# The first 64 score bursts of a transformer block in another order: four query groups per key tile, projections by row tile, the norm in pieces

## The chip, the cores and the metric

The kernel runs on one core of one Trainium2 chip. The metric is the device time of one execution in microseconds. Before the change it is 1097.61 us, the median of 3 runs (1097.25 to 1097.75).

## What is computed

One pre-norm transformer block in bf16, with x of 2048 rows by 1024 columns. Attention has 32 query heads of 32 columns and one key and value head that all of them share; the second half is a gated feed-forward part of width 3584. Cut to what matters:

```python
def attention(x):
    q = (x @ wq).reshape(B, S, 32, 32).transpose(0, 2, 1, 3)
    k, v = x @ wk, x @ wv
    scores = einsum("bhqd,bkd->bhqk", q, k) * 32 ** -0.5
    o = einsum("bhqk,bkd->bhqd", softmax(scores), v)
    return o.transpose(0, 2, 1, 3).reshape(B, S, 1024) @ wo

def ffn(x):
    return (sigmoid(x @ w_gate) * (x @ w_up)) @ w_down

h  = x + attention(layernorm(x))
h2 = h + ffn(layernorm(h))
```

## The kernel before, in words

**Tiles and bursts.** The rows are 16 tiles of 128. Eight chunks of four heads make up the 1024 query columns (a "q" below is 128 columns, four heads). A *unit* is two row tiles (256 rows); there are eight units, and the feed-forward part goes by unit too. The scores of one row tile are worked in *bursts*: in one burst TensorE makes four score matmuls, one per head on its own 32 rows of the array, into two pairs of PSUM banks of `S_ps` (L727 to L752). ScalarE then takes the exponential of each pair in one instruction of 128 x 1024 (`one_exp`, L757 to L772). There are 512 bursts, so 1024 exponentials. `ORDER` (L128) lists the groups of eight bursts; there are 64 groups `g`.

**Narrow and wide groups.** The groups from the ninth on are wide: one burst is one key tile against four q of one row tile (512 columns per matmul), and a group is one half of the keys. The first eight groups (row tiles 0 and 1) are narrow: a burst is two key tiles against two q (eight matmuls of 256 columns, L744 to L752), and a group goes over all keys.

**Probabilities times V, and the sums.** `pv_group` (narrow, L979) and `pv_wide` (L885) multiply the probabilities by V, four heads on four column strips of the array. The sum of each row of probabilities comes in one of two ways. For groups 0 to 2 (`G_SUM = 3`) TensorE multiplies the same probabilities by ones (L1017). For the others VectorE first adds tiles pairwise (`add_pair`, L843; `run` and `merge`, L861 and L870, or L820 and L832 where wide), and TensorE multiplies only the last result by ones (L999, or L933 where wide). VectorE then copies the product out, inverts the sum through two 32x32 transposes and multiplies (L1038 to L1050, or L905, L908, L955 to L966).

**The head.** Up to the 25th burst the order is written out by hand: the first three groups go together (`HG = 3`), each taking key tiles 2p and 2p+1 in turn, and the strings of `HEAD` (L125) say what is put between the bursts: V projections, query projections, the norm of a row tile, pieces of the first product with V. `k_group` (L569) projects two key tiles at a time (256 columns) and ScalarE copies the result out (L576). `vq_group` (L610) projects two q for one row tile, or V for two tiles; the copies of query groups 0 and of some others go to ScalarE (L632, L652), the others and V's to VectorE (L639, L636). `q_group` (L645) projects one q for 256 or 512 rows (L654). Where TensorE would wait, `keep_busy` (L334) puts in matmuls of zeros (L346).

**The first layernorm** is made tile by tile: statistics (`ln1_stats`, L427: two of L431 and one of L436), subtraction (L458) and multiplication (L463) on VectorE, the power on GpSimd, then a DMA transpose on SP's queue (L553). The calls are written out in the head, two to three tiles ahead of what the bursts need. `LOADS` (L425) says after which tile's transpose SP's queue loads which further tile of x; x tiles 4 to 7 and the first three pieces of wq are asked for at the start (L270 to L273).

**The main loop** (L1583 to L1690) runs from the 26th burst on. It keeps a clock for each engine from costs in the code (L135 and the second argument of each `inc`), and picks the next thing for TensorE: the next burst once the exponentials before it are done by that clock, else products with V as `PV_PLAN` allows, else `next_group` (L1352): the output projection with wo (L1104), then query projections, then gate, up and down of the feed-forward part. All of these use the two banks of `X_ps`; a group takes a bank in `open_group` and gives it back when it has been copied out (`run_item`, L350 to L365). VectorE's work that may wait stands in a list (`put`, L1066), from which `dve_fill` (L1072) takes what fits before the next copy.

**Where the probabilities wait** for V: a ring of 18 tiles in `Pr`, and in the head also parts of `hact`, `wo` and `QT` that are not yet in use (`p_tile`, L708). wo is loaded, and the later columns of `QT` are written, when the products with V have come 16 bursts far (L1590, L648).

Of the kernel before, what the change touches and what calls it, by code (L numbers as in the profile page):

```python
# [8 lines left out]
F32 = mybir.dt.float32  # L9
# [75 lines left out]
def bass_sequential_preLN__grouped_kv_mqa__glu_gated_glu__prompt_kernel(  # L85
# [43 lines left out]
    ORDER += [(t_, i_) for t_ in range(2, NT) for i_ in range(NQ // 2)]  # L129
    UNITS = [[t_, t_ + 1] for t_ in range(0, NT, TPQ)]  # L130
# [3 lines left out]
    WD_AT, WD_GAP, WD_LATE = 6, 4, 10  # L134
# [5 lines left out]
    with ExitStack() as es:  # L140
# [99 lines left out]
        def _(unused):  # L240
# [70 lines left out]
            I_US, I_MAX = 4.0, 210  # L311

            def by_columns(g):
# [10 lines left out]
                return pe_mode[0] == "s" and (more or n < NQC * NQ and k[0] >= min(BPG * (n + 1) + 1, NB - (n == NQC * NQ - 1)))  # L324
# [100 lines left out]
            LOADS = {3: (8,), 4: (9,), 5: ("q3", 10), 6: (11,), 7: (12, 13), 9: (14,), 11: (15,)}  # L425
# [43 lines left out]
            def ln1_out(t):  # L469
                xnT_read[t] = xnT_val[t] = transposed(sp, xnT_tile(t), xn(t), t % 4, xn_val[t])  # L470
                for i in LOADS.get(t, ()):
                    if i == "q3":
                        load_wq(3, 768, 256)
                    else:
                        load_x(i)
# [93 lines left out]
            def k_group(p, mid=None):  # L569
                c0 = 2 * p * P  # L570

                def evac(bank, tick):
                    if mid is not None:
                        mid()
                    need(act, tick)
                    k_val[p] = c_act.inc(act.activation(out=kT4[:, c0:c0 + 256], in_=bank[:, 0:256], func=ACTF.Copy), 0.33, 0.1)  # L576
                    return k_val[p]
                items = mm_list([(wk4[:, dt, :], xnT[:, p, dt, :]) for dt in range(DT)],
# [1143 lines left out]
```

## Time and profile before

| What | Number |
|---|---|
| median of 3 runs | 1097.61 us |
| span of the profiled execution, first to last instruction | 1094.1 us |
| TensorE, matmuls | 1075.0 us, 98% of the span |
| ScalarE | 1007.0 us, 92% |
| VectorE | 897.4 us, 82% |
| GpSimd | 65.8 us, 6% |
| HBM read and written | 161.61 MB and 4.19 MB |

The profile holds one execution, whose span is 1094.1 us; the time of a run is taken around the whole program, and the median of the runs is 3.5 us above the span. Rows of the profile give the line of the kernel, the engine, what is written and read, the shapes, the count, the busy time and the mean of one. A matmul's duration contains its way through the array, which the next one overlaps: sixteen matmuls in a row take far less than sixteen durations, and what counts is the distance from start to start.

### The profile page before, as it was taken

To read this page: it belongs to the slowest core of one execution; us is meant where nothing else is said; L and a number is where in the kernel's file an instruction comes from. 1 tells how busy PE (TensorE), PEld (TensorE's weight loads), DVE (VectorE), ACT (ScalarE), POOL (GpSimd) and SP (SyncE) were. 2 spreads that over 40 slices of the span, in tenths; PEclk is the share of its full clock that TensorE was granted. 3 is DMA by queue.
4 is the path that set the end of the run, shared out by engine and by line. 5 is a ranking of instruction groups with operands and counts; after the bars stand their busy time and mean duration, and the time that the engine had idled before them with its cause. 6 is when DMAs were issued, how large, how long until landed. Compare 5 with 4: busy or idle time off the path is not lost. (4 is left out here: it accounts for less than half of the span.)

```text
span 1094.1 us, 33732 instructions
## 1 busy us (share of the span) xinstructions
PE 1075.0 (98%) x14751; PEld 632.2 (58%) x14804; DVE 897.4 (82%) x1494; ACT 1007.0 (92%) x1155; POOL 65.8 (6%) x136
## 2 busy tenths in 40 slices
PE   8999999999999999999999999999999999999999
PEld 7564466644666356643666347653666447653884
DVE  7769997889988989799989899898888899798321
ACT  6999999999999999999999999999999999999110
POOL 4500110100000000000000000000000000000000
PEclk9999999999999999999999999999999999999999
DMA  9842528950976549670997719670697509872570
GB/s 209 163 116 81 127 70 244 258 131 24 245 212 191 118 109 250 197 205 21 242 244 206 154 31 275 193 179 25 167 263 215 126 22 269 232 197 71 149 175 20
DMA packets 332418, 175.84 MB, mean 161 GB/s; under 512 B 39536, under 2 KB 326512, under 8 KB 332272
## 3 DMA queue, kind: packets, MB, share of 16 engines
q1 hardware_dynamic: 326464, 163.47, 58.8%
q0 software_dynamic: 2544, 9.44, 2.7%
q8 instruction: 116, 1.90, 0.8%
q10 hardware_dynamic: 3264, 0.79, 0.4%
q14 instruction: 30, 0.25, 0.1%
HBM read 161.61 MB, written 4.19 MB: 152 GB/s over the span
## 5 line engine op out<-in xcount | busy, mean ns | idle before, releaser
L770 ACT ACTIVATE Pr<-S_ps 128x1024 bf16<-128x1024 f32 x992 | 943.6, 1204 | 3.2 <-PE S_ps L747 1.4
L820 DVE TENSOR_TENSOR pairs<-Pr 128x1024 bf16<-128x1024 bf16 x446 | 303.8, 684 | 28.7 <-ACT Pr L770 27.9
L832 DVE TENSOR_TENSOR pairs<-pairs 128x1024 bf16<-128x1024 bf16 x390 | 269.0, 690 | 11.4
L328 PE MATMUL X_ps<-QT,wgu 128*128 128x128 bf16 (+1 forms) x2263 | 209.5, 243 | 1.3 <-DMA wgu<-in_B_w_gate_dram 1.2
L328 PEld LDWEIGHTS X_ps<-QT,wgu 128*128 128x128 bf16 x2263 | 163.9, 98 | 39.5 <-issue 25.9
L737 PE MATMUL S_ps<-QT,kT 32*128 32x512 bf16 x1792 | 176.8, 385 | 1.5 <-ACT Pr L770 0.9
L328 PE MATMUL X_ps<-zone,hact 128*128 128x512 bf16 (+2 forms) x652 | 150.0, 371 | 4.4 <-issue 3.8
L328 PE MATMUL X_ps<-QT 128*128 128x128 bf16 (+1 forms) x1652 | 153.1, 242 | 0.2
L328 PEld LDWEIGHTS X_ps<-QT 128*128 128x128 bf16 x1652 | 119.9, 98 | 25.8 <-issue 15.6
L1253 ACT ACTIVATE gu<-X_ps 128x512 f32<-128x512 f32 x112 | 86.9, 776 | 45.7 <-PE X_ps L328 45.6
L737 PEld LDWEIGHTS S_ps<-QT,kT 32*128 32x128 bf16 x1792 | 45.0, 91 | 135.1 <-ACT Pr L770 123.9
L1274 DVE SCALAR_TENSOR_TENSOR hact<-gu,X_ps 128x512 bf16<-128x512 f32 x112 | 76.6, 684 | 48.7 <-PE X_ps L328 47.5
L894 PE MATMUL X_ps<-Pr,V 128*32 128x512 bf16 x1792 | 114.8, 381 | 0.4
L328 PEld LDWEIGHTS X_ps<-zone,hact 128*128 128x128 bf16 x686 | 59.2, 98 | 73.9 <-issue 18.5
L894 PEld LDWEIGHTS X_ps<-Pr,V 128*32 128x32 bf16 x1792 | 41.5, 96 | 48.5 <-issue 14.0
L330 PE MATMUL X_ps<-zone,hact 128*32 128x512 bf16 x952 | 61.3, 380 | 0.0
L328 PE MATMUL X_ps<-zone 128*128 128x512 bf16 (+3 forms) x506 | 60.2, 264 | 1.0 <-ACT kT L576 0.4
L399 POOL CAST mean<-mv 128x1 f32<-128x1 bf16 x28 | 8.7, 310 | 816.1 <-DVE mv L1145 804.2
L328 PE MATMUL X_ps<-wo,QT 128*128 128x512 bf16 x213 | 53.7, 380 | 1.4 <-issue 0.6
L330 PE MATMUL X_ps<-QT,wgu 128*32 128x256 bf16 (+1 forms) x1636 | 50.8, 264 | 0.0
L328 PEld LDWEIGHTS X_ps<-zone 128*128 128x128 bf16 x506 | 32.6, 97 | 22.5 <-issue 7.9
L330 PEld LDWEIGHTS X_ps<-QT,wgu 128*32 128x32 bf16 x1636 | 38.9, 97 | 11.2 <-issue 6.6
(108 smaller groups left out, 720.8 us busy)
## 6 DMA issues: line engine op xcount, KB each, us to landing
wgu<-in_B_w_up_dram SPq DMA_DIRECT2D x81, 512.0 KB, 5.6
wgu<-in_B_w_gate_dram SPq DMA_DIRECT2D x72, 512.0 KB, 5.7
QT<-in_B_w_gate_dram SPq DMA_DIRECT2D x57, 512.0 KB, 5.5
QT<-in_B_w_up_dram SPq DMA_DIRECT2D x48, 512.0 KB, 6.7
zone<-in_B_w_down_dram POOLq DMA_DIRECT2D x14, 512.0 KB, 6.2
out_dram<-hx SPq DMA_DIRECT2D x31, 128.0 KB, 1.7
hx<-in_A_x_dram SPq DMA_DIRECT2D x15, 256.0 KB, 2.8
Pr<-in_B_w_gate_dram SPq DMA_DIRECT2D x5, 512.0 KB, 7.2
```

What stands on the lines that cost most here:

```text
L328: return pe.matmul(out, lhsT=lhsT, rhs=rhs, start=start, stop=stop, skip_group_check=main[0])
L330: ins = pe.matmul(out[DH * j:DH * (j + 1)], lhsT=lhsT[:, DH * j:DH * (j + 1)], rhs=rhs, start=start, stop=stop, tile_position=(0, DH * j), ...
L399: return c_pool.inc(pool.tensor_copy(out=mean[:, i:i + 1], in_=mv[:, i:i + 1, 0]), 0.2)
L737: ins = pe.matmul(S_ps[:, ((2 * k + j // 2) % 3) * 2 + j % 2, :], lhsT=kT4[DH * j:DH * (j + 1), kt * P:(kt + 1) * P], rhs=QT[DH * j:DH * ( ...
L770: c_e.inc(act.activation(out=p_tile(k, n % 2), in_=S_ps[:, 2 * pr:2 * pr + 2, :].rearrange("p a (b q) -> p (a b) q", q=QC), func=ACTF.Exp, ...
L820: slot_use[x] = c_dve.inc(dve.tensor_tensor(out=dst(x), in0=p_tile(k - 1, hh), in1=p_tile(k, hh), op=ALU.add), T_ADD, 0.08)
L832: slot_use[x] = slot_use[y] = c_dve.inc(dve.tensor_tensor(out=pairs[:, x, :], in0=pairs[:, x, :], in1=pairs[:, y, :], op=ALU.add), T_ADD, ...
L894: ins = pe.matmul(bank[DH * j:DH * (j + 1), :], lhsT=V[:, kt, :], rhs=p_tile(k, j // 2)[:, j % 2 * 2:j % 2 * 2 + 2, :], start=b == 0, stop ...
L1253: tanh_val[n] = c_act.inc(act.activation(out=slot, in_=bank, func=ACTF.Tanh, scale=0.5), T_TANH, 0.1)
L1274: gu_read[n] = c_dve.inc(dve.scalar_tensor_tensor(out=hact[:, 2 * fs[0]:2 * fs[0] + ft, r0:r0 + len(ts) * P], in0=slot.rearrange("p (a b) ...
```

## The change

**Order of the bursts.** All groups are wide now. Groups 0 to 3 are row tiles 0 and 1 against the first half of the keys, for q 0 to 3 and q 4 to 7. They take each key tile in turn (after two key tiles each at the very start); groups 4 to 7 are the second half of the keys, one group after the other. Products with V of groups 0 to 3 come in two chunks of four bursts each, the sums likewise, and `OLP` and `OLS`, which lie in parts of `hact` and `hx`, hold what has been added up until the second half is there.

**Sums.** `SUM_PLAN = "ppppdddp"`: of the first eight groups, TensorE makes the sums of five by itself, and VectorE adds for three.

**Projections.** Keys are projected tile by tile (128 columns) and copied out by VectorE, but for the first two; queries of row tiles 0 and 1 two q at a time; rows 256 to 511 one q at a time. No table: `TODO` is a list of priorities, of which `head_group` takes the first whose inputs are there by the kernel's clock. The main loop runs from the first burst on, and `keep_busy` is not reached in it.

**Norm.** The layernorm of tiles 2 to 15 stands in VectorE's list in four pieces per tile. x tiles 4 and 5 are loaded after tile 2's transpose, 6 and 7 after tile 3's, and so on; the fourth piece of wq is asked for at the start.

**Ring and constants.** The places for the probabilities are given out by a first-in-first-out list over `Pr`, `wo` and `QT` (9, 4 and 4 bursts). The plans and thresholds of the main loop have other values.

```diff
-    NEAR = 1
-    PV_PLAN = "aaacabaaacadaaaAadaaaAaAdAadaaaaadbbaaaDbaaaaaaacbbaaaaDaabCbAaa"
-    WO_PLAN = "aaaaaaba"
-    PV_HOLD = 1.0
-    BANK_WAIT = 0.15
-    G_SUM, NPB = 3, 4
-    HG = 3
-    HEAD = ['u', 'Vu', 'L', '', 'VULu', 'u', 'VPP', 'wL', 'LzPULz', 'zPLz', 'W', 'LzP', 'PPzL', 'VVL', 'PPV', '', 'UPP', 'UP', 'PV', 'U', 'PU', '', '', '']
+    NEAR = 2
+    PV_PLAN = "BDaeeaaaAbbaaBbaAEeAababaAbBeAaaEAAaeDbdeaAbbbaEDabAAabaAaaabaAaacbcabDa"
+    WO_PLAN = "bbabaaaa"
+    PV_HOLD = 0.75
+    BANK_WAIT = 0
+    G_SUM, HCH, HB0 = 4, 4, 2
+    LN_LEAD = 2
+    SUM_PLAN = "ppppdddp"
     K_BUSY = 10
-    HEAD_U = [5, 6, 7, 4]
-    ORDER = [(0, 0), (0, 1), (0, 2), (1, 0), (0, 3), (1, 1), (1, 2), (1, 3)]
+    TODO = ["k1", "k0", "q1a", "q1b", "q0a", "q0d", "q0c", "q0b", "k2", "q1d", "k5", "k4", "ka", "v1", "v0", "k7",
+            "q1c", "v3", "v2", "k3", "k6", "kc", "kf", "kd", "kb", "ke", "v4", "v7", "v5", "k8", "v6", "Q2",
+            "k9"]
+    ORDER = [(0, 0), (1, 0), (0, 2), (1, 2), (0, 1), (0, 3), (1, 1), (1, 3)]
+    BURST = [(g_, b_) for g_ in range(G_SUM) for b_ in range(HB0)]
+    BURST += [(g_, b_) for b_ in range(HB0, BPG) for g_ in range(G_SUM)]
+    BURST += [(g_, b_) for g_ in range(G_SUM, NQC * NQ) for b_ in range(BPG)]
+    CHUNKS = [(g_, tuple(range(b_, b_ + HCH))) for b_ in range(0, BPG, HCH) for g_ in range(G_SUM)]
+    CHUNKS += [(g_, tuple(range(BPG))) for g_ in range(G_SUM, NQC * NQ)]
...
-            load_wq(1, 256, 256)
-            load_wq(2, 512, 256)
-            for t in range(4, 8):
-                load_x(t)
+            for i in range(1, 4):
+                load_wq(i, 256 * i, 256)
...
-            LOADS = {3: (8,), 4: (9,), 5: ("q3", 10), 6: (11,), 7: (12, 13), 9: (14,), 11: (15,)}
+            LOADS = {2: (4, 5), 3: (6, 7), 4: (8, 9), 5: (10, 11), 6: (12,), 7: (13,), 8: (14,), 9: (15,)}
...
+            def k_group(tiles, on_act=False):
...
+                    if on_act:
+                        v = c_act.inc(act.activation(out=kT4[:, c0:c0 + n], in_=bank[:, 0:n], func=ACTF.Copy), 0.1 + n * 0.0009, 0.1)
+                    else:
+                        v = c_dve.inc(dve.tensor_copy(out=kT4[:, c0:c0 + n], in_=bank[:, 0:n]), 0.12 + n * 0.00104, 0.08)
...
             def summed(g):
-                return g >= G_SUM
+                return g >= len(SUM_PLAN) or SUM_PLAN[g] == "d"
...
+            place, before = [], {}
+            fifo = collections.deque([(("Q", i), None) for i in range(4)] + [(("W", i), None) for i in range(4)] +
+                                     [(("P", i), None) for i in range(RP // 2)])
...
+            QT_FREE = max(use(kk_) for kk_ in range(NB) if place[kk_][0] == "Q") + 1
+            HEAD_FREE = max(use(kk_) for kk_ in range(NB) if place[kk_][0] != "P") + 1
...
+            room = [hact_flat[:, i * 1024:(i + 1) * 1024].bitcast(F32) for i in (0, 1, 2, 3, 6)]
+            OLP = [room[0], olp[:], room[1], room[4]]
+            OLS = [room[2], hx[:, 2, :].bitcast(F32), room[3], hx[:, 3, :].bitcast(F32)]
...
+                    if head and x % 2 == 0:
+                        need(dve, tick, ols_val[u])
+                        if bs[0] == 0:
+                            ins = dve.tensor_copy(out=OLS[u], in_=bank)
+                        else:
+                            ins = dve.tensor_tensor(out=OLS[u], in0=bank, in1=OLS[u], op=ALU.add)
...
+            def ln1_all(t):
+                chain = "m%d" % (t % 2)
...
+                put(chain, 0.45, lambda: ln1_sub(t), had(mean_val, lambda: None if t >= 4 and t - 4 not in xnT_read else
+                                                         when(mean_val[t], xnT_read.get(t - 4))))
...
+            for t in range(2, NT):
+                ln1_all(t)
...
+            def spare_dve():
+                return len(xn_val) >= min(NT, (k[0] // 4 if k[0] < NHB else k[0] - NHB + BPG) + LN_LEAD)
+
+            def head_group(now, kinds="kvqQ"):
+                for i, x in enumerate(todo):
...
+                    if ok:
+                        del todo[i]
+                        if x[0] == "k":
+                            return k_group(x[1], x[1][0] < K_ACT)
...
+                if todo and not busy(cur[0]) and min(bank_time(b) for b in range(2)) <= k_pe[0] + 0.1:
+                    cur[0] = head_group(k_pe[0], "k")
+                    if busy(cur[0]):
+                        run_group(cur[0])
+                        idle = 0
+                        continue
```

More of the change, by code (lines that the diff above doesn't have):

```diff
@@ new lines, in _ @@
+            for kk_ in range(NB):
+                while True:
+                    if not fifo:
+                        fifo.append((place[CONS[used]], CONS[used]))
+                        used += 1
+                    x_ = fifo.popleft()
+                    if x_[0][0] == "P" or kk_ < NHB:
+                        break
+                place.append(x_[0])
+                before[kk_] = x_[1]
+            QT_FREE = max(use(kk_) for kk_ in range(NB) if place[kk_][0] == "Q") + 1
+            HEAD_FREE = max(use(kk_) for kk_ in range(NB) if place[kk_][0] != "P") + 1
@@ L940, in fs, with fd @@
                     return r
[L941 to L943 removed]
+                if not plain:
+                    items.append((0.217, fs, sum_time))
+                alone = [BURST_NO[g, b] for b in bs] if plain else range(NB - 2, NB) if final else []
+                for n, kx in enumerate(alone):
+                    def fd(bank, n=n, kx=kx):
                         need(pe, (c_e, 2 * kx + 2))
@@ L1064, in _ @@
+            head_left = [None]
             lo = []
```

700 lines of the change are left out of this document (272 added, 428 removed).

## The prediction

> **What bounds the kernel now.** I read the page first.
>
> ```profile
> span 1094.1 us, 33732 instructions
> PE 1075.0 (98%) x14751; PEld 632.2 (58%) x14804; DVE 897.4 (82%) x1494; ACT 1007.0 (92%) x1155; POOL 65.8 (6%) x136
> ```
>
> Two engines are over 90%, so shares alone decide nothing. The second view is the table of busy times by stretch: the stretch, its length, the busy time of each engine, the granted clock, the DMA share.
>
> ```profile
> 10.00:30.00 20.00, 17.11 (x296) 13.72 (x294) 18.18 (x46) 15.10 (x21) 10.49 (x24) 1.00 0.97 202
> 30.00:60.00 30.00, 27.51 (x443) 17.02 (x440) 19.19 (x45) 29.56 (x39) 12.51 (x28) 1.00 0.84 168
> 60.00:70.00 10.00, 9.52 (x248) 6.70 (x248) 4.12 (x11) 9.93 (x12) 0.00 (x0) 1.00 0.39 92
> 70.00:130.00 60.00, 59.92 (x1012) 28.88 (x1006) 57.48 (x107) 59.91 (x66) 5.64 (x9) 1.00 0.41 112
> 200.00:1000.00 800.00, 791.67 (x10686) 448.41 (x10731) 702.85 (x1126) 798.34 (x912) 25.89 (x49) 1.00 0.65 170
> 1011.00:1094.00 83.00, 80.68 (x840) 62.20 (x840) 19.85 (x32) 8.36 (x14) 1.29 (x3) 1.00 0.47 117
> ```
>
> From 200 to 1000 us ScalarE is busy 798.3 of 800 and TensorE 791.7. Both are full; the question is which of them the end waits for. The third view answers it: the instructions in order of time near the last exponential (start, length, line, what, how many).
>
> ```profile
> 960.48 1.03 PE L328 MATMUL X_ps<-wo,QT 128*128 128x512 bf16 x4
> ...
> 1009.35 1.68 PE L330 MATMUL X_ps<-zone,hact 128*32 128x512 bf16 x28
> ...
> 1014.75 1.95 PE L328 MATMUL X_ps<-QT 128*128 128x128 bf16 x32
> 1016.54 3.62 PE L328 MATMUL X_ps<-wo,QT 128*128 128x512 bf16 x15
> ```
>
> ```profile
> 999.60 11.30 ACT L770 ACTIVATE Pr<-S_ps 128x1024 bf16<-128x1024 f32 x12
> ```
>
> Row tile 14's output projection (`wo,QT`) starts at 960.5 us, so its feed-forward work could follow after a norm. Yet at 1009 us TensorE is still at the down projection of the unit before (`zone,hact`), and tile 14's gate matmuls begin at 1014.75, when ScalarE's last exponential (999.60 + 11.30 = 1010.9) is already over. TensorE had work lying ready for tens of microseconds. So **the end is set by TensorE's total work plus its idle time**; the exponentials are a second chain, nearly as long, that runs ahead of it. What the head is worth is read from TensorE in the head. From 10 to 70 us it idles 2.89 + 2.49 + 0.48 = 5.9 us, against 0.1 from 70 to 130. And part of its busy time there is filler:
>
> ```profile
> L346 PE MATMUL X_ps<-pairs 128*128 128x128 bf16 x79 | 5.6, 219 | 0.8 <-ACT QT L632 0.8
> ```
>
> These are 79 matmuls of zeros, 5.6 us. **Idle and filler together, 11.5 us of the head carry no work.** A better order of the same work can win no more than that there.
>
> **The change, part by part.**
>
> *Idle and filler: -11.5 us at most.* First the pace of the key tiles, from ScalarE in order of time (idle before it, and who ended it, in brackets).
>
> ```profile
> 15.76 1.94 ACT L770 ACTIVATE Pr<-S_ps 128x1024 bf16<-128x1024 f32 x2 [1.16 <-PE S_ps L747]
> ...
> 22.52 0.38 ACT L576 ACTIVATE kT<-X_ps 128x256 bf16<-128x256 f32 x1 [1.80 <-PE X_ps L328]
> 22.80 1.02 ACT L770 ACTIVATE Pr<-S_ps 128x1024 bf16<-128x1024 f32 x1
> ```
>
> Two exponentials start 1.94 - 1.02 = 0.92 us apart. Now three bursts (six exponentials) use two key tiles, 2.8 us per tile. In the new order a key tile serves four bursts, 7.4 us. The norm may keep a slower pace, and TensorE can go on to later rows meanwhile. Whether there is work enough: by 78 us, 16 q-pieces of 512 rows (rows 0 to 1023) at 8 x 0.22 us = 28 us, keys and V some 13, 36 bursts at 0.39, seven chunks of eight sets at 0.219 (both priced below) 14 + 12. That is 67 us for the 66 between 12 and 78, so TensorE can be full, but early on little of it is ready. The loads of x tiles 4 to 7 move behind the transposes of tiles 2 and 3 on SP's queue, the fourth piece of wq ahead of them. Key tile 4 is due at the 17th burst, near 42 us, and that covers it; with the old pace each late tile would stop ScalarE, as at 22.52.
>
> *More matmuls for sums: +3.0 us.* Groups 0 to 2 make their sums with ones matmuls of 256 columns; group by group:
>
> ```profile
> L1017 PE MATMUL X_ps<-hact,ones 128*32 128x256 bf16 x64 | 4.3, 280 | 0.3 <-DVE V L636 0.3
> L1017 PE MATMUL X_ps<-Pr,ones 128*32 128x256 bf16 x64 | 3.7, 274 | 0.0
> L1017 PE MATMUL X_ps<-wo,ones 128*32 128x256 bf16 x32 | 1.9, 275 | 0.0
> L1017 PE MATMUL X_ps<-QT,ones 128*32 128x256 bf16 x32 | 1.9, 274 | 0.0
> L999 PE MATMUL X_ps<-pairs,ones 128*32 128x256 bf16 x40 | 2.8, 275 | 0.0
> L737 PE MATMUL S_ps<-QT,kT 32*128 32x512 bf16 x1792 | 176.8, 385 | 1.5 <-ACT Pr L770 0.9
> ```
>
> The L1017 rows make 192 matmuls, 48 sets of four strips. The distance from set to set comes from the order of time:
>
> ```profile
> 64.68 0.28 PE L1017 MATMUL X_ps<-hact,ones 128*32 128x256 bf16 x4
> ...
> 65.77 0.28 PE L1017 MATMUL X_ps<-Pr,ones 128*32 128x256 bf16 x4
> ...
> 951.74 1.91 PE L894 MATMUL X_ps<-Pr,V 128*32 128x512 bf16 x32
> ```
>
> Ten sets lie between the first two (ones and V alternate): 0.109 us each. The wide form needs (1.91 - 0.38) / 7 = 0.219 per set of 512 columns. So 48 x 0.109 = 5.2 us go, and five groups x 8 bursts x 0.219 = 8.8 come. Merged sums fall from 10 sets x 0.109 = 1.1 to 3 x 0.219 = 0.7. Together 8.8 - 5.2 - 0.4 = +3.2, and I take 3.0, since some of the ones matmuls can stand where TensorE would wait.
>
> *Products with V and scores: 0.* The same columns: two sets of 0.109 against one of 0.219; a burst stays 176.8 / 448 = 0.39 us.
>
> *Projections by row tile: 0.*
>
> ```profile
> 21.45 1.03 PE L328 MATMUL X_ps<-zone 128*128 128x256 bf16 x8 [0.27 <-DMA zone<-hn]
> 1026.25 1.95 PE L328 MATMUL X_ps<-QT 128*128 128x128 bf16 x32
> ```
>
> (1.03 - 0.27) / 7 = 0.108 us for 256 columns (0.27 is the length of one), (1.95 - 0.22) / 31 = 0.056 for 128. Two small ones cost 0.004 more than a large one, 0.3 us for all 64 of the keys.
>
> *ScalarE's copies: 0 on this path.* Most key and query copies leave it; that shortens the other chain (rival 2 prices it).
>
> *What TensorE still waits in the new head: +5.0 us.* The trace of before can't show this, so it has two ends. The good end is the stretch of 70 to 130, 0.08 us of 60. The bad end is that nothing is won, 11.5. The nearest row is 30 to 60 us, where few fillers are left and TensorE waits for tiles and copies: 2.49 of 30, 8%, or 5.0 of 60. I take 5.0, as the new head has the same norm to wait for early on, and no fillers.
>
> *VectorE: in those 5.0 as long as its copies are prompt.* It takes 14 key copies, and each chunk is copied out once for the product and once for the sum:
>
> ```profile
> L636 DVE CAST V<-X_ps 128x64 bf16<-128x64 f32 x8 | 1.7, 218 | 5.2 <-PE X_ps L328 5.2
> L639 DVE CAST QT<-X_ps 128x256 bf16<-128x256 f32 x4 | 1.7, 420 | 0.7 <-PE X_ps L328 0.7
> L905 DVE COPY olp<-X_ps 128x512 f32<-128x512 f32 x28 | 19.3, 688 | 4.8 <-PE X_ps L894 4.3
> 12.00:78.00 66.00, 47.26 (x111) 1.00 0.70 144
> ```
>
> A key copy lies between the first two rows, 0.22 and 0.42, say 0.28: 14 x 0.28 = 3.9 us. Seven chunks by 78 us make 14 x 0.69 = 9.7, in place of some 5 for narrow groups. Earlier query copies add about 4. From 47.3 (last row: VectorE's busy time in those 66 us) it comes to some 60 of 66. Queued behind a waiting copy are the norm's pieces and the sums, and for the bank that it empties waits TensorE. The Trainium skill, "TensorEngine Tiling (Array Packing)", section "PSUM Bottleneck", says that tiling speeds up TensorE but not the copies out of PSUM, and advises using ScalarE and VectorE both; the change goes the other way, and rival 3 is what that would mean here.
>
> *Plans and thresholds of the main loop: 0.* TensorE idles 8.3 of 800 us from 200 to 1000. New letters can win no more than that, and may lose as much; nothing in the trace says which.
>
> Sum: -11.5 + 3.0 + 5.0 = -3.5. The span goes from 1094.1 to 1090.6, and with the 3.5 us that lie between the span and the median of 1097.6, the time is **1094.1 us**.
>
> **The rivals.**
>
> 1. *The forecast.* With waits of 0.1 to 8.3 it gives 1089.2 to 1097.4.
>
> 2. *The exponentials set the end after all.* For it: ScalarE is busy 798.3 of 800 us. Against: TensorE's ready work at 1010 us. Its gain would be the copies taken away (some 11, each moving the next exponential by 22.80 - 22.52 = 0.28 us: 3.1) and the idle (1.16 and 1.80 in the rows above, some 0.5 in smaller pieces), less about 0.6 for a later first burst, which needs four q and so a second piece of wq. That is -5.9, **1091.7 us**.
>
> 3. *Slower: VectorE's copies hold the two banks.* The place is 12 to 78 us. Some 38 short groups (14 of keys, 8 of V, 16 halves of chunks) last 0.4 to 0.9 us, and each can find VectorE inside a piece of 0.68 us; a wait of half of that, 0.34, makes 13 us in place of 5.0: +8, **1102 us**. It decides as soon as VectorE is over nine tenths busy there, against 47.3 / 66 = 72% now. Against it: `dve_fill` leaves room before a copy that it expects.
>
> 4. *The head only moves its waits.* TensorE waits 8.5 us in other places, and the time stays at **1097.6 us**. Part of this is that the order may not come about as written: `TODO` is by what is ready, and the first burst's fourth q stands late in it.
>
> 5. *TensorE's clock falls.* The 64 matmuls at the very start lie 0.10 us apart, those after them 0.056, though the clock column reads 1.00 throughout.
>
> ```profile
> 1.11 6.60 PE L487 MATMUL X_ps<-pairs 128*128 128x128 bf16 x64 [1.11 <-DVE pairs L278]
> ```
>
> Without fillers the early head could fall back to the slow pace. From 10 to 30 us 17.1 busy less 5.6 filler leaves 11.5 us of work, which would take up to 11.5 more, less the 2.9 of idle that this fills: +8.6, **1103 us**. Against it: real groups stand where fillers stood. The Trainium skill, "TensorE: Matmul & The Clock Gate", section "Why this matters for your kernels", warns of idle gaps over about 3 us; no gap in these rows is near that.
>
> **How the numbers follow.** Differences under 0.2% (2.2 us, so 1095.4 to 1099.8) count as the same, about what a measurement of this kernel can tell from none. Chances: the forecast 0.48 (0.38 of it below 1095.4, 0.10 the same), rival 2 0.14, rival 4 0.13 (0.03 faster, 0.08 the same, 0.02 slower), rivals 3 and 5 together 0.25. Faster 0.55, same 0.18, slower 0.27. The forecast with rivals 2 and 4 holds 0.75 and needs 1088.5 to 1099 when the plans give or take 1 us; to leave out no more than 0.2 the range has to reach into rival 3, to 1102. So the range is 1088.5 to 1102.0, and the likeliest case's own is 1089.2 to 1097.4.
>
> **What would show it.** In the stretch table: TensorE idle 5 us from 10 to 70 us with no row of zeros matmuls there, and ScalarE near 10 of 10 from 30 us on. Ones matmuls in 40 sets of 512 columns, 8.8 us. VectorE at some 60 of 66 from 12 to 78. The last exponential some 6 us earlier, near 1005, and the stretch after it *longer* than 83 us: that is the sign that TensorE and not ScalarE sets the end. If it stays at 83 us, rival 2 is right. The forecast is wrong if TensorE idles over 10 us in the head, or if its idle from 200 to 1000 us differs from 8.3 by more than 3.

## The result, and the profile after

The changed kernel takes 1100.23 us (median of 11 runs, 1097.94 to 1101.92) against 1096.86 us (11 runs, 1095.34 to 1100.51). The ratio is 1.003, with a 95% interval of 1.0019 to 1.004: slower by some 3.4 us, where the prediction had said 3.5 us faster.

The page of the changed kernel first: its span, and the busy time of each engine.

```profile
span 1099.0 us, 34241 instructions
PE 1070.7 (97%) x15024; PEld 618.1 (56%) x15076; DVE 895.4 (81%) x1485; ACT 1003.7 (91%) x1145; POOL 63.8 (6%) x136
```

TensorE is busy for 4.3 us less than before, and yet the span is 4.9 us longer. The table by stretch has the same stretches as in the prediction (length, busy time of PE, PEld, DVE, ACT and POOL, granted clock, DMA share, GB/s):

```profile
10.00:30.00 20.00, 19.15 (x280) 14.85 (x280) 16.70 (x44) 17.56 (x23) 6.12 (x14) 1.00 0.76 173
30.00:60.00 30.00, 27.42 (x561) 13.96 (x561) 26.88 (x63) 30.00 (x34) 12.84 (x31) 1.00 0.63 123
60.00:70.00 10.00, 9.79 (x233) 4.51 (x228) 6.89 (x16) 9.74 (x12) 3.38 (x8) 1.00 0.45 84
70.00:130.00 60.00, 59.50 (x823) 22.82 (x815) 53.23 (x89) 59.93 (x66) 4.38 (x8) 1.00 0.49 133
200.00:1000.00 800.00, 789.07 (x11178) 447.35 (x11221) 700.23 (x1123) 798.02 (x912) 24.62 (x49) 1.00 0.63 163
1011.00:1094.00 83.00, 82.48 (x853) 61.98 (x854) 20.07 (x32) 10.80 (x17) 1.29 (x3) 1.00 0.46 120
```

In the head all went well. TensorE idles 0.85 + 2.58 + 0.21 = 3.6 us from 10 to 70 us, with no fillers, and ScalarE is full from 30 us on. ScalarE's groups from 10 to 78 us show the gain (what is written, how many, busy time). In the kernel before there are 31 + 16 + 8 + 8 = 63 exponentials:

```profile
L770 ACT ACTIVATE Pr<-S_ps 128x1024 bf16<-128x1024 f32 x31 | 30.0, 1077 | 1.4 <-PE S_ps L747 1.4
L770 ACT ACTIVATE hact<-S_ps 128x1024 bf16<-128x1024 f32 x16 | 15.8, 1057 | 0.6 <-PE S_ps L747 0.5
L770 ACT ACTIVATE QT<-S_ps 128x1024 bf16<-128x1024 f32 x8 | 8.7, 1113 | 0.0
L770 ACT ACTIVATE wo<-S_ps 128x1024 bf16<-128x1024 f32 x8 | 8.2, 1042 | 0.0
```

In the changed kernel there are 38 + 16 + 16 = 70 in the same time:

```profile
L768 ACT ACTIVATE Pr<-S_ps 128x1024 bf16<-128x1024 f32 x38 | 36.0, 1135 | 0.0
L768 ACT ACTIVATE wo<-S_ps 128x1024 bf16<-128x1024 f32 x16 | 15.3, 1091 | 0.3 <-PE S_ps L748 0.3
L768 ACT ACTIVATE QT<-S_ps 128x1024 bf16<-128x1024 f32 x16 | 15.1, 1075 | 0.3 <-PE S_ps L748 0.3
```

Seven exponentials of about 0.9 us each make a lead of 6 us. At the end it is gone, and more: the last exponential ends at 989.47 + 23.97 = 1013.4 us, 2.5 us *later* than before.

```profile
989.47 23.97 ACT L768 ACTIVATE Pr<-S_ps 128x1024 bf16<-128x1024 f32 x26
```

From 200 to 1000 us nothing explains that (idle 10.9 us for 8.3). The loss lies in a stretch that the prediction's table had left out, 130 to 200 us, where the feed-forward part begins:

```profile
156.00:159.00 3.00, 0.00 (x0) 0.00 (x0) 2.93 (x6) 2.06 (x3) 0.00 (x0) 1.00 1.17 138
159.00:162.40 3.40, 0.00 (x0) 0.00 (x0) 1.57 (x3) 0.00 (x0) 0.00 (x0) 0.56 0.35 88
162.40:166.00 3.60, 3.59 (x32) 2.96 (x33) 0.59 (x1) 1.65 (x2) 0.00 (x0) 0.50 0.00 0
```

TensorE stands still from 156 to 162.4 us, ScalarE from about 158, and then TensorE works for 3.6 us at half its clock. In the kernel before, the same 6.4 us held 5.80 us of TensorE's work at a clock of 1.00:

```profile
156.00:162.40 6.40, 5.80 (x120) 4.67 (x108) 6.26 (x11) 6.40 (x9) 0.72 (x1) 1.00 0.73 136
```

The instructions of the changed kernel in order of time tell why (idle before, and what ended it, in brackets):

```profile
151.54 1.49 POOL L260 DMA_DIRECT2D zone<-in_B_w_down_dram  x2
...
152.19 1.24 SPq L564 DMA_TRANSPOSE QT<-hn  x1
...
155.37 0.40 PE L748 MATMUL S_ps<-QT,kT 32*128 32x512 bf16 x4 [0.42 <-ACT Pr L768]
...
162.41 1.36 PE L342 MATMUL X_ps<-QT,zone 128*128 128x128 bf16 x11 [6.64 <-DMA QT<-hn]
...
164.35 1.94 ACT L768 ACTIVATE Pr<-S_ps 128x1024 bf16<-128x1024 f32 x2 [6.28 <-PE S_ps L748]
```

GpSimd issues two loads of w_down (numbers 6 and 7, 512 KB each) at 151.5 and 152.3 us, and SP the transpose of hn of row tile 1 at 152.2. The gate matmuls of tile 1 wait for the transpose at the head of TensorE's queue, the next score burst waits behind them, and ScalarE waits for the burst. The view of the DMA issues gives the times to landing, for 150 to 156 us:

```profile
zone<-in_B_w_down_dram POOLq DMA_DIRECT2D x2, 512.0 KB, 7.6
QT<-hn SPq DMA_TRANSPOSE x1, 10.2
```

The transpose takes 10.2 us. In the kernel before it took 5.9, and one load left 0.66 us ahead of it:

```profile
QT<-hn SPq DMA_TRANSPOSE x1, 5.9
```

Why two loads now: `load_wd` holds a load back by exponentials only from number `NFP - WD_LATE` on, with `NFP` = 14. `WD_LATE` went from 10 to 6, so loads 4 to 7 aren't held any more, and load 7 follows load 6 at once. In the kernel before, loads 6 and 7 left only at 160.0 and 167.8 us.

**First theory.** The head brings what it should, and 156 to 167 us takes it back: the stop, and the half clock after it. **Rivals.** The loss is spread over the main loop with its new plans; or the clock makes most of it; or the exponentials, not TensorE, set the end.

### The profile page after: what moved, and what is told of

Its sections match the earlier page's. It is cut to its first block, busy times and chain, and to the rows that moved or that the text cites. A ratio compares the mean times of both kernels' runs of the same rounds, so it can differ in the third digit from the quotient of the medians.

```text
span 1099.0 us, 34241 instructions
## 1 busy us (share of the span) xinstructions
PE 1070.7 (97%) x15024; PEld 618.1 (56%) x15076; DVE 895.4 (81%) x1485; ACT 1003.7 (91%) x1145; POOL 63.8 (6%) x136
## 4 chain that ended last, share of the span: by engine, by line
PE 79%; ACT 10%; DMA 4%; DVE 3%; issue 3%; POOL 1%; SPq 0%; ACTq 0%; DVEq 0%
PE X_ps L342 43%; PE X_ps L344 14%; PE S_ps L748 12%; PE X_ps L855 9%; ACT Pr L768 8%; DMA QT<-hn 2%; DMA wgu<-in_B_w_up_dram 1%; DMA zone<-in_A_wq_dram 1%; ACT QT L768 1%; PE X_ps L902 1%; ACT wo L768 1%; PE X_ps L917 0%; DVE pairs L805 0%; DMA zone<-hn 0%; POOL sd L424 0%
## 5 line engine op out<-in xcount | busy, mean ns | idle before, releaser
L805 DVE TENSOR_TENSOR pairs<-Pr 128x1024 bf16<-128x1024 bf16 x470 | 320.3, 683 | 27.5 <-ACT Pr L768 27.1
L817 DVE TENSOR_TENSOR pairs<-pairs 128x1024 bf16<-128x1024 bf16 x408 | 281.4, 690 | 11.8
L748 PE MATMUL S_ps<-QT,kT 32*128 32x512 bf16 x2048 | 202.2, 385 | 4.3 <-ACT Pr L768 2.9
L342 PE MATMUL X_ps<-QT,wgu 128*128 128x128 bf16 (+1 forms) x2073 | 197.0, 245 | 2.4 <-DMA QT<-hn 1.2
L342 PE MATMUL X_ps<-zone,hact 128*128 128x512 bf16 (+2 forms) x599 | 137.0, 370 | 4.6 <-issue 4.0
L855 PE MATMUL X_ps<-Pr,V 128*32 128x512 bf16 x1984 | 128.0, 381 | 0.3 <-issue 0.3
L344 PE MATMUL X_ps<-zone,hact 128*32 128x512 bf16 x1152 | 72.3, 380 | 0.0
L344 PE MATMUL X_ps<-QT,wgu 128*32 128x256 bf16 (+1 forms) x2076 | 63.6, 264 | 0.0
L342 PE MATMUL X_ps<-zone 128*128 128x128 bf16 (+3 forms) x442 | 45.0, 250 | 0.6 <-DMA zone<-in_A_wq_dram 0.5
L344 PEld LDWEIGHTS X_ps<-zone,hact 128*32 128x32 bf16 x1152 | 28.8, 96 | 29.3 <-issue 5.9
```

The source lines that it names most:

```text
L342: return pe.matmul(out, lhsT=lhsT, rhs=rhs, start=start, stop=stop, skip_group_check=main[0])
L344: ins = pe.matmul(out[DH * j:DH * (j + 1)], lhsT=lhsT[:, DH * j:DH * (j + 1)], rhs=rhs, start=start, stop=stop, tile_position=(0, DH * j), ...
L748: ins = pe.matmul(S_ps[:, ((2 * k + j // 2) % 3) * 2 + j % 2, :], lhsT=kT4[DH * j:DH * (j + 1), kt * P:(kt + 1) * P], rhs=QT[DH * j:DH * ( ...
L805: slot_use[x] = c_dve.inc(dve.tensor_tensor(out=dst(x), in0=p_tile(k - 1, hh), in1=p_tile(k, hh), op=ALU.add), T_ADD, 0.08)
L817: slot_use[x] = slot_use[y] = c_dve.inc(dve.tensor_tensor(out=pairs[:, x, :], in0=pairs[:, x, :], in1=pairs[:, y, :], op=ALU.add), T_ADD, ...
L855: ins = pe.matmul(bank[DH * j:DH * (j + 1), :], lhsT=V[:, kt, :], rhs=p_tile(kx, j // 2)[:, j % 2 * 2:j % 2 * 2 + 2, :], start=b == bs[0], ...
```

## The experiments

| Label | Median, us | Ratio to before, 95% interval |
|---|---|---|
| changed kernel | 1100.23 | 1.0019 to 1.004 |
| e1_late10 | 1093.86 | 0.9954 to 0.9979 |
| e2_hold | 1092.12 | 0.9948 to 0.9975 |
| b_late6 | 1101.13 | 1.0027 to 1.0054 |
| e4_zeros | 1097.62 | 0.9995 to 1.0012 |
| e9_one | 1093.74 | 0.9959 to 0.9982 |
| e5_sums | 1093.25 | 0.995 to 0.9975 |
| e6_tanh | 1087.93 | 0.9897 to 0.9924 |
| e7_thr | 1109.46 | 1.0088 to 1.0119 |
| e10_pe | 1092.33 | 0.9946 to 0.9969 |
| b_tanh | 1090.84 | 0.9935 to 0.9961 |
| b_few | 1099.18 | 1.0012 to 1.0041 |
| e11_copies | 1094.49 | 0.9972 to 0.999 |

The kernel before took 1096.9 to 1097.6 us beside them. Labels with e are made from the changed kernel, those with b from the kernel before.

### One constant put back: e1_late10

```diff
-    WD_FROM, WD_GAP, WD_LATE = 10, 4, 6
+    WD_FROM, WD_GAP, WD_LATE = 10, 4, 10
```

> The changed kernel with one constant put back: WD_LATE = 10, so that w_down's load number 7 waits for exponentials on GpSimd's queue again. Theory (the gain of the head is lost at 156 to 167 us, where the transposes of hn of tile 1 take 10.2 us beside loads 6 and 7): load 7 leaves some 8 us later, the transposes land in about 6 us as in the kernel before, TensorE's stop of 6.6 us shrinks to about 2.5 and its clock stays at 1.00, so 1100.2 - 4 - 2 = about 1094 us. First rival (the loss is spread over the retuned main loop, idle 10.9 for 8.3 us, and the end): 1098 or more. Second rival (the fall of the clock is most of the loss): also about 1094, told apart by the run with warming matmuls.

1093.86 us: 6.4 us come back with one constant. TensorE is busy for 5.68 us of the 6.4 from 156 to 162.4 us again, at a clock of 1.00. The transpose, from the DMA issues:

```profile
QT<-hn SPq DMA_TRANSPOSE x1, 3.1
```

One detail was missed: the transpose took 3.1 us, not 6. The loads are held from number 4 on, which moves number 5 to 146.67 us and number 6 to 154.49, so that only number 6 still leaves beside the transpose, 0.6 us before it lands (151.99 + 3.1 = 155.1). The first rival (1098 or more) falls.

### The two loads held back: e2_hold

```diff
-                if wd_next[0] >= NFP - WD_LATE:
+                if wd_next[0] >= 6:
                     need(pool, (c_e, 2 * k[0] - 2))
...
-                if wd_free and wo_val[0] and k[0] >= wd_at[0] and when(*wd_free[0][1]) <= k_pe[0]:
+                if wd_free and wo_val[0] and k[0] >= wd_at[0] and when(*wd_free[0][1]) <= k_pe[0] and (
+                        wd_next[0] < 6 or 1 in hnT_val and when(hnT_val[1]) <= k_pe[0]):
```

> The changed kernel with w_down's loads 6 and 7 held back until the transposes of hn of tile 1 should have landed. Theory: nothing large runs beside the transposes, they land in 3 to 4 us, no stop of TensorE at 156 us, mean clock 1.000 for 0.997, and the gain of the head shows: 1100.2 - 6.6 - 2 = about 1091.5 us, faster than before by some 5 us. First rival (loss spread over the main loop): 1098 or more although the stop is gone. Third rival (the end is set by ScalarE's exponentials, not by TensorE's sum): what ScalarE starved, 6.3 us, comes back, 1094.

1092.12 us, faster than both kernels: 8.1 us under the changed one and, by the interval, 0.25% to 0.52% under the one before. The transpose lands after 3.0 us, the stop is gone, and the last exponential ends at 979.83 + 24.88 = 1004.7 us, 8.7 us earlier than with the stop (the same stretch, and ScalarE in order of time):

```profile
156.00:162.40 6.40, 5.68 (x92) 4.58 (x90) 6.29 (x11) 6.40 (x8) 0.75 (x1) 1.00 0.46 127
```

```profile
979.83 24.88 ACT L768 ACTIVATE Pr<-S_ps 128x1024 bf16<-128x1024 f32 x27
```

The theory had said 1091.5 and its third rival (the exponentials set the end) 1094. This run doesn't tell these two apart.

### The same constant in the kernel before: b_late6

```diff
-    WD_AT, WD_GAP, WD_LATE = 6, 4, 10
+    WD_AT, WD_GAP, WD_LATE = 6, 4, 6
```

> The kernel before with one constant of the change: WD_LATE = 6 for 10, so that w_down's load 7 isn't held by exponentials. Theory: load 7 follows load 6 at about 154 us, beside the transposes of hn of tile 1 (issued at 154.9, landed after 5.9 us); if they now take 10 us the gate matmuls of tile 1 wait some 3 to 4 us and the time goes to about 1100 to 1103; if load 7 still leaves later than the transposes, 1097 as before and the collision needs the earlier hand-over as well. First rival: 1097, and no stop at this place.

1101.13 us. With nothing else of the change in it, the constant makes the kernel before slower by 3.7 us. Three loads leave from 154.70 us on, the transpose takes 8.5 us, and TensorE and ScalarE stop. TensorE's wait (us, times, longest), the transpose, and the stretch from 162.4 to 167 us:

```profile
PE X_ps L328 <- DMA QT<-hn: 2.3, 1, 2.3
```

```profile
QT<-hn SPq DMA_TRANSPOSE x1, 8.5
```

```profile
162.40:167.00 4.60, 3.08 (x38) 2.46 (x39) 3.31 (x6) 2.24 (x3) 0.00 (x0) 0.80 0.52 172
```

### Only one load held back: e9_one

```diff
-                if wd_next[0] >= 6:
+                if wd_next[0] >= 7:
...
-                        wd_next[0] < 6 or 1 in hnT_val and when(hnT_val[1]) <= k_pe[0]):
+                        wd_next[0] < 7 or 1 in hnT_val and when(hnT_val[1]) <= k_pe[0]):
```

> The changed kernel with only w_down's load 7 held back (until the transposes of hn of tile 1 should have landed, and by exponentials); load 6 still leaves at 151.5 us, just ahead of the transposes. Theory (each load beside the transposes lengthens them: 3.0 us with none, 5.9 with one in the kernel before, 8.5 to 10.2 with a second one behind them): they land after about 6 us, at 158, TensorE stops for about 2.3 us, under the 3 us after which the clock fell, and the time is about 1092.1 + 2.5 = 1094.5 us. Rival (one load beside them is as bad as two): about 1100. Rival (only the load behind the transposes does harm): 3 us, no stop, 1092.

1093.74 us. The transpose, and TensorE's wait for it (1.4 us, where 2.3 were expected):

```profile
QT<-hn SPq DMA_TRANSPOSE x1, 4.9
```

```profile
PE X_ps L342 <- DMA QT<-hn: 1.4, 1, 1.4
```

The intervals of e2_hold and e9_one overlap, so the 1.4 us of stop show in the trace but not with certainty in the time. Over all runs the transpose takes 3.0 and 3.1 us with no load beside it but for the last 0.6 us of e1_late10, 4.9 and 5.9 with one, 8.5 to 10.2 with two or three.

### The stop without the idle: e4_zeros

```diff
+                    if g.warm:
+                        open_group(g)
+                        mode("f")
+                        for i in range(g.warm):
+                            pe.matmul(X_ps[:, g.bank, 0:P], lhsT=kT4[:, 0:P], rhs=kT4[:, 0:P], start=True, stop=True,
+                                      skip_group_check=True)
...
+                g.warm = 110 if n == 2 else 0
```

> The changed kernel with 110 matmuls of 128 columns without use (about 6 us at full clock) put ahead of the wait for the transposes of hn of tile 1, so that TensorE isn't idle in the stop; the wait itself and ScalarE's starving stay. Theory: only the part of the loss that the clock at 0.50 makes comes back, about 2 us: 1098. Second rival (the fall of the clock is most of the loss): 1094 or less.

1097.62 us, 2.6 less. The rows show TensorE at full pace after the wait (eleven gate matmuls in 0.78 us, 1.36 above) and ScalarE still starved:

```profile
155.06 6.32 PE L374 MATMUL X_ps<-kT 128*128 128x128 bf16 x110
161.21 0.78 PE L343 MATMUL X_ps<-QT,zone 128*128 128x128 bf16 x11
...
162.35 1.94 ACT L776 ACTIVATE Pr<-S_ps 128x1024 bf16<-128x1024 f32 x2 [4.92 <-PE S_ps L756]
```

The transpose landed after 8.7 us this time, which takes 6.28 - 4.92 = 1.4 us off the stop; so the clock's own part lies between 1.2 and 2.6 us, and the wait is most of the loss.

### Less work for TensorE in the head: e5_sums

From here on the labels with e have e2_hold as their base.

```diff
-                            ins = pe.matmul(bank[DH * j:DH * (j + 1), :], lhsT=ones[:],
-                                            rhs=p_tile(kx, j // 2)[:, j % 2 * 2:j % 2 * 2 + 2, :],
+                            few = plain and n > 0
+                            ins = pe.matmul(bank[DH * j:DH * (j + 1), 0:32] if few else bank[DH * j:DH * (j + 1), :], lhsT=ones[:],
+                                            rhs=p_tile(kx, j // 2)[:, j % 2 * 2, 0:32] if few else p_tile(kx, j // 2)[:, j % 2 * 2:j % 2 * 2 + 2, :],
```

> The kernel with both loads held, in which 31 of the 40 sets of ones matmuls of the first groups go over 32 columns in place of 512 (the sums leave out the other columns of those bursts); order, waits and everything else stay. Those sets take some 0.03 to 0.05 us instead of 0.219, together 5.3 to 5.8 us less on TensorE. Theory (TensorE's total work sets the end, so the matmuls that came with the change cost their full time): 1092.1 - 5.5 = about 1086.6 us. Rival (they stand where TensorE would wait for exponentials or the norm anyway): TensorE idles instead, 1090 to 1092.

1093.25 us: nothing comes back, against the theory's 1086.6. TensorE has less to do and waits for exponentials instead. The stretch from 70 to 140 us and TensorE's waits for exponentials over the whole span, first in e2_hold:

```profile
70.00:140.00 70.00, 69.39 (x957) 27.14 (x950) 60.83 (x103) 69.08 (x76) 6.34 (x11) 1.00 0.47 129
```

```profile
PE S_ps L748 <- ACT Pr L768: 3.6, 8, 0.9
```

Then in e5_sums:

```profile
70.00:140.00 70.00, 66.89 (x955) 26.57 (x952) 60.63 (x104) 69.03 (x76) 6.88 (x11) 1.00 0.47 129
```

```profile
PE S_ps L748 <- ACT Pr L768: 6.2, 14, 0.9
```

So the theory that TensorE's total sets the end falls for the head; e10_pe asks the same of the main loop.

### Less work for ScalarE: e6_tanh

```diff
-                        tanh_val[n] = c_act.inc(act.activation(out=slot, in_=bank, func=ACTF.Tanh, scale=0.5), T_TANH, 0.1)
+                        tanh_val[n] = c_act.inc(act.activation(out=slot[:, 0:256] if n >= NGU else slot,
+                                                               in_=bank[:, 0:256] if n >= NGU else bank, func=ACTF.Tanh, scale=0.5), T_TANH, 0.1)
```

> The kernel with both loads held, in which every tanh after the first four goes over 256 columns in place of 512 (the rest of its tile keeps older values); order and waits stay. ScalarE has some 0.2 us less for each of some 94 tanh before the last exponential, about 19 us of its chain. Theory (TensorE's total sets the end; its idle from 200 to 1000 us is 9.3 us, of which its waits for exponentials are under 1): 1091 to 1092. Rival (the exponentials set the end): the last exponential comes earlier and the time falls by what TensorE can give up of its idle, 5 to 9 us: 1083 to 1087.

1087.93 us. The rival is right in kind: with shorter tanh the last exponential ends at 979.21 + 21.26 = 1000.5 us, 4.2 us earlier than in e2_hold, and the median is lower by as much. Of some 19 us cut only these are won; after that TensorE is full (796.6 of 800) and ScalarE waits for it:

```profile
979.21 21.26 ACT L768 ACTIVATE Pr<-S_ps 128x1024 bf16<-128x1024 f32 x23
```

```profile
200.00:1000.00 800.00, 796.60 (x11207) 447.09 (x11199) 703.27 (x1130) 791.41 (x916) 24.15 (x48) 1.00 0.61 161
```

ScalarE's waits for scores over the whole span, first in e2_hold, then here:

```profile
ACT Pr L768 <- PE S_ps L748: 1.1, 3, 0.8
```

```profile
ACT Pr L768 <- PE S_ps L748: 5.7, 15, 0.9
```

The gain is under the 5 to 9 us of the expectation because TensorE's idle of 9.3 us, from which these were taken, was not all idle. The trace of e2_hold lacks some matmuls: its page has 15024 for 15076 weight loads. In e9_one, whose page has 15076 of each, TensorE is busy 796.2 of these 800 us, so it had 3.8 us to give up. A shorter tanh also empties its bank earlier. That this is the gain is unlikely: in e2_hold no matmul's wait of 0.2 us or more is put down to a tanh, only weight loads' waits, 2.1 us in all (0.2 here). The run by itself doesn't separate the two; e11_copies, which touches no bank, does.

**The new theory:** the order in which TensorE takes bursts and other work is fixed when the kernel is built. ScalarE's exponentials pace it, TensorE is a few us behind them, and the end is the last exponential plus the work that the order has put behind it.

### Three thresholds put back: e7_thr

```diff
-    NEAR = 2
-    PV_HOLD = 0.75
-    BANK_WAIT = 0
+    NEAR = 1
+    PV_HOLD = 1.0
+    BANK_WAIT = 0.15
```

> The kernel with both loads held and three thresholds of the main loop as in the kernel before (NEAR 1, PV_HOLD 1.0, BANK_WAIT 0.15), the plans as in the changed one. It tests the step that cost plans and thresholds at nothing. If they are worth nothing, 1092 give or take 1. Theory now (one value decides where each transfer and each group lands, and a plan fits only the thresholds it was made with): worse, 1094 to 1105, with new stops of TensorE or ScalarE in the main loop that the waits show. Rival: the new thresholds cost something and the old ones give 1089 to 1091.

1109.46 us, 17 us more: new stops all over the main loop, for both engines. From 200 to 1000 us TensorE idles 16.9 us (3.8 in e9_one, which has the changed kernel's thresholds; both pages have as many matmuls as weight loads) and ScalarE 7.4 (0.7 in e2_hold). Another late transpose isn't the cause, as TensorE waits only 0.4 us for one there.

```profile
200.00:1000.00 800.00, 783.09 (x10753) 436.34 (x10749) 695.08 (x1113) 792.56 (x904) 23.98 (x48) 1.00 0.60 156
```

The reading is that the letters of the plan fit the thresholds they stand with; which of the three does it wasn't tested. Such values can't be costed at nothing: three of them are worth three times what the new head wins.

### Less work for TensorE in the main loop: e10_pe

```diff
-                        ins = pe.matmul(bank[DH * j:DH * (j + 1), :], lhsT=ones[:],
-                                        rhs=pairs[:, sum_wide[(g, j // 2)], j % 2 * 512:(j % 2 + 1) * 512],
+                        w = 512 if final else 32
+                        ins = pe.matmul(bank[DH * j:DH * (j + 1), 0:w], lhsT=ones[:],
+                                        rhs=pairs[:, sum_wide[(g, j // 2)], j % 2 * 512:j % 2 * 512 + w],
```

> The kernel with both loads held, in which the ones matmuls on VectorE's merged sums go over 32 columns in place of 512, except the very last (the sums leave out the other columns): 30 sets from 92 us to the end of the exponentials, each 0.219 us less some 0.04, so about 5.5 us less on TensorE in the main loop; order and waits stay. It is the counterpart of the run with shorter tanh (19 us less on ScalarE gave 4.2 us). New theory (with a fixed order the exponentials pace TensorE, which is at most some 4 us behind them): nothing comes back, 1091 to 1093. The prediction's theory (TensorE's total sets the end): 1086.5.

1092.33 us, as e2_hold. The matmuls did get shorter; the row of this group has 12.3 us for 124 matmuls in the changed kernel, and here:

```profile
L903 PE MATMUL X_ps<-pairs,ones 128*32 128x32 bf16 x120 | 5.9, 188 | 0.1
```

Some 6 us less on TensorE give nothing, as the new theory says, and not the 5.5 of the prediction's.

### Less work for ScalarE in the kernel before: b_tanh

The edit of e6_tanh, in the kernel before.

> The kernel before with every tanh after the first four over 256 columns in place of 512 (the rest of its tile keeps older values); order and waits stay. It asks what set the end before the change. The prediction's theory (TensorE's total work and idle): 1096 to 1097, at most 1 us. New theory (the exponentials set the pace in this kernel too): as with the shorter tanh in the changed kernel, about 4 us: 1093, and the last exponential earlier by as much.

1090.84 us, 6.1 less (by the interval, 4.3 to 7.1). In the profiled executions the last exponential ends at 1007.2, 3.7 us earlier than the 1010.9 of before:

```profile
984.23 23.02 ACT L770 ACTIVATE Pr<-S_ps 128x1024 bf16<-128x1024 f32 x25
```

So the exponentials paced the kernel before too.

### The fillers taken out of the kernel before: b_few

```diff
                 for i in range(n):
-                    pe.matmul(X_ps[:, b, 0:P], lhsT=warm[:, 0:P], rhs=warm[:, 0:P], start=True, stop=True,
-                              skip_group_check=True)
+                    if i < 1:
+                        pe.matmul(X_ps[:, b, 0:P], lhsT=warm[:, 0:P], rhs=warm[:, 0:P], start=True, stop=True,
+                                  skip_group_check=True)
                     k_pe[0] += 0.058
```

> The kernel before with one matmul of zeros where keep_busy puts in several (the clocks of the planner, and so the order, stay): most of the 79 fillers and 5.6 us of TensorE's busy time go. It tests the fillers' part of the term of 11.5 us. If they only stand where TensorE waits for ScalarE: 1097, its idle from 10 to 70 us up by about 5 us. If some of them delay what comes after them: faster by up to 2. If the clock falls without them (a rival of the prediction): slower, with a clock below 1.00 from 10 to 40 us.

1099.18 us, 2.2 more. The third case came: the clock falls.

```profile
30.00:40.00 10.00, 9.34 (x124) 6.93 (x121) 5.70 (x14) 7.31 (x10) 3.33 (x8) 0.74 0.75 165
```

The zeros carried no work, but they paid for themselves. The new head has none, real groups stand in their places, and its clock is 1.00 throughout.

### More work for ScalarE in the head: e11_copies

```diff
                         v = c_dve.inc(dve.tensor_copy(out=kT4[:, c0:c0 + n], in_=bank[:, 0:n]), 0.12 + n * 0.00104, 0.08)
+                        need(act, const_val)
+                        for x in (rs, mean):
+                            act.activation(out=x[:, NT + tiles[0]:NT + tiles[0] + 1], in_=ones[:, 0:1], func=ACTF.Copy)
```

> The kernel with both loads held, and 28 small copies without use on ScalarE in the head, two beside VectorE's copy of each key tile from the third on; the order of TensorE and all waits stay. It doubles what the change took from ScalarE. The smallest copy of a trace so far, of 128 columns, takes 0.28 us, and moves the next exponential by as much; copies of one column should take less, some 0.15 to 0.25 us, together 4 to 7 us. New theory (the exponentials set the pace): the last exponential and the end come later by as much, 1096 to 1099, and TensorE idles more in the head. The prediction's step (ScalarE's copies are worth nothing on the path that sets the end): 1092.

1094.49 us, 2.4 more than e2_hold. The copies were shorter than estimated. In order of time:

```profile
19.63 0.23 ACT L606 ACTIVATE rs<-ones 128x1 f32<-128x1 bf16 x1
19.72 0.22 ACT L606 ACTIVATE mean<-ones 128x1 f32<-128x1 bf16 x1
19.82 1.04 ACT L771 ACTIVATE QT<-S_ps 128x1024 bf16<-128x1024 f32 x1
```

A pair delays the next exponential by 19.82 - 19.63 = 0.19 us; 14 pairs make 2.7 us. The size of the expectation was missed (4 to 7). The direction was met: work put on ScalarE in the head comes out at the end. How much of it does is less sure, as in the profiled executions the last exponential comes 1.6 us later (973.78 + 32.48 = 1006.3, after 1004.7), and the intervals of e2_hold and this run overlap a little (0.9948 to 0.9975, and 0.9972 to 0.9990).

## Why the prediction was wrong

*"Plans and thresholds of the main loop: 0."* **This step turned the sign.** `WD_LATE` was among the values costed at nothing. It takes the wait away from loads 4 to 7, of which 6 and 7 had kept out of the transpose's way. With it the changed kernel takes 1100.2 us, with the old value 1093.9; the old kernel goes from 1097.4 to 1101.1 with the new value alone. The step argued from the idle time of 200 to 1000 us and said that new letters could win or lose 8.3 us there. That stretch did stay within its bound (10.9), though neither figure is all idle: the page of the kernel before has 14751 matmuls for 14804 weight loads, that of the changed one 15024 for 15076, and where none is missing (e9_one) the idle reads 3.8. Nor did it bound what such values can lose: three thresholds put 16.9 us of idle there (e7_thr). The loss of the changed kernel was at 156 us, in a stretch that no step had priced and none of the prediction's signs covered; and a transfer that may leave earlier was not set against the transfers it would then meet.

*"The end is set by TensorE's total work plus its idle time."* **Wrong, though its sum came near.** Some 5 to 6 us taken from TensorE gave nothing, in the head (e5_sums) or in the main loop (e10_pe). Work taken from ScalarE gave 4.2 us in the new kernel and 6.1 in the old, and 2.7 us of work added to it cost 2.4. A view of the kernel before fits: from 200 to 1000 us ScalarE waits for scores only three times, 1.4 us in all. The reading behind the step was that TensorE had ready work left at 1010 us. It had (the hn of tile 14 left for its transpose at 977.4 us), but the order in its queue doesn't let it take that work earlier: the bursts stand between. Ready work shows that another order could fill TensorE, not that TensorE sets the end of this one.

*The sign that should have told the two apart* was no sign: the stretch after the last exponential. It is 83.2 us in the kernel before and in b_tanh, and 85.6 or 85.7 in the changed kernel, e2_hold, e6_tanh and e11_copies, whichever engine was made faster. It belongs to the order.

*"ScalarE's copies: 0 on this path", and rival 2.* The copies were on the path. Rival 2 added them up as 3.1 us, with the idle 3.5 less 0.6: -5.9, or 1091.7 us. Without the collision the time is 1092.1 us, and the last exponential 1010.9 - 1004.7 = 6.2 us earlier. Two of its terms can be read off: from 10 to 78 us ScalarE makes 10 copies fewer (rival 2 said 11) and idles 2.6 us less (e2_hold against before; rival 2 said 2.9, net of the later start). Rival 2 was the right account of the head, and it was given a chance of 0.14. Its own sign, a last stretch of 83 us, did not come: that stretch is 2.4 us longer, so the profiled span is only 3.8 us shorter where the medians differ by 5.3. The two don't have to agree. Every run's time lies 1.7 to 2.8 us above its own span; the prediction's 3.5 us are more, so the profiled execution of the kernel before must have been faster than the three runs of the median.

*Idle and filler, -11.5, and waits of the new head, +5.0.* As bookkeeping of TensorE these held: the idle is 3.6 us (5.0 forecast), and no fillers are left. But they aren't what was won; TensorE's time came free where ScalarE sets the pace.

*More matmuls for sums, +3.0.* They came (TensorE's sums of the first groups). e5_sums shows that they cost no time where they stand. The 2.4 us by which the stretch after the last exponential became longer may be the work that they pushed behind it; that is argued, not shown.

*VectorE, 60 of 66 us from 12 to 78:* 52.9, so rival 3 never came near. *Rival 4* fell, as the lead by 78 us shows. *Rival 5*, the clock: the fall itself is real (b_few), but the new head is full enough. The fall came at 159 us instead, as the result of a stop.

On that fall the Trainium skill, "TensorE: Matmul & The Clock Gate", section "What's actually happening", says that the clock goes to half after an idle window of about 3.4 us and comes back after as long a busy one. The trace agrees: TensorE stopped at 155.8 us, the clock was 1.00 up to 159 and 0.56 on average from 159 to 162.4; work began again at 162.4, and the clock was 0.50 up to 166 and 1.00 after it.

What the forecast got right by luck: 1094.1 us is within 2 us of the kernel without the collision. Two errors, a wrong bound and a free constant, stood in it side by side.

## What to carry to other kernels

When a change lets a transfer start earlier, list what else is in flight then, and above all a short transfer that the head of an in-order queue waits for; one constant here was worth more than the change around it. Where an order is fixed when the kernel is built and two engines are both near full, find out which one paces it by shortening each in turn, since ready work in a trace doesn't tell. And put the whole span into the table of stretches: what lies between two of them is where a loss can hide.

## What the runs showed of the hardware

The transpose of one row tile (128 x 1024, bf16) from SP's queue took 3.0 us alone (e2_hold) and up to 10.2 us beside 512 KB loads from GpSimd's queue. In the changed kernel the load asked for 0.65 us ahead of it landed after 5.2 us, the one behind it after 10.0. The Trainium skill, "DMA: Bandwidth & Descriptors", section "Queues, rings and completion order", says that each DMA engine takes turns between its queues packet by packet. The lengthening from 3.0 to 10.2 us fits that, but no run here shows the turns themselves.

The clock can fall without a long gap. In b_few no wait of TensorE in the early head is over 1.3 us, yet after some 4 us with under a third of its time busy (0.20, 0.31, 0.27 and 0.44 us of each) the clock halved. In b_late6 the longest stop was 2.3 us, and the clock was 0.80 on average in the 4.6 us after 162.4. For b_few, the last two of the four, and the two after them, stretch by stretch:

```profile
26.00:27.00 1.00, 0.27 (x6) 0.10 (x1) 1.00 (x3) 1.00 (x2) 0.88 (x2) 1.00 1.16 262
27.00:28.00 1.00, 0.44 (x5) 0.42 (x6) 0.97 (x4) 0.49 (x1) 0.55 (x2) 1.00 0.77 120
28.00:29.00 1.00, 0.76 (x7) 0.39 (x4) 0.96 (x3) 0.31 (x2) 0.92 (x3) 0.70 0.96 253
29.00:30.00 1.00, 0.78 (x17) 0.41 (x18) 0.96 (x3) 1.00 (x3) 0.70 (x2) 0.50 1.06 353
```
